# Where the matmuls' operands lie: the rows of x and h of an RWKV + gated-MLP kernel moved to multiples of 2048 bytes

## Chip, cores and metric

One Trainium2 chip, one of its cores. The metric is the device time of one execution in microseconds (us), inputs in HBM to output in HBM. Three runs of the kernel before took 540.85, 543.45 and 539.7 us; the median is 540.85.

## What is computed

An RWKV-style recurrence over 768 steps for 4 batches and 8 heads of 48 channels gives `y`; its heads side by side are the 384 channels of `x` for 3072 tokens, and a gated MLP of inner width 1536 follows. All in float32.

```python
for t in range(S):                                   # S = 768
    kt, vt, rt = k[:, :, t], v[:, :, t], r[:, :, t]
    cur = einsum('bhd,bhe->bhde', u[None] * kt, vt)
    y[:, :, t] = einsum('bhd,bhde->bhe', rt, state + cur)
    state = w[None, :, :, None] * state + einsum('bhd,bhe->bhde', kt, vt)
x = y.transpose(0, 2, 1, 3).reshape(3072, 384)
out = (sigmoid(x @ w_gate) * (x @ w_val)) @ w_out    # 384 -> 1536 -> 384
```

## The kernel before

**The recurrence** is done in 12 chunks of 64 tokens, each in two groups of heads (24 groups). A group's small matmuls (48 or 64 rows, 48 or 64 columns, float32) are those of `scores` (line 348), `outer` (L403) and `into_y` (L320); they read `chan`, `dec`, `toks`, `score` and `state`. Two chunks make a tile `xt` of 512 tokens; there are six tiles of tokens.

**Float32 by parts.** x, the weights and the inner h are each split into a high and a low part of type float32r (`x_high` L456 and `x_low` L460 on ScalarE and VectorE; `h_high` L520 on ScalarE, `h_low` L524 mostly on GpSimd; the weights once, L236 to L253). A product is then three matmuls (`PASS`): low weights with high x, high with high, high weights with low x.

**The MLP.** For each tile of tokens and each of 12 slices `f` of the inner width, `Moe.up` issues 18 matmuls (L502: gate and value, three k tiles, three passes) of a 128x128 weight and 512 columns of `xt` into a PSUM bank of the pool `ring`. Then come the sigmoid (L511, ScalarE), the product (L515, VectorE), `h_high` and `h_low`; and `Moe.down`, one slice later, issues 9 matmuls (L540) of 512 columns of `h` into the three banks `acc`. An item (one tile, one slice) is thus 27 large matmuls. The first tile's first two slices are done in halves of 256 columns; in the last tile the third output bank is done in two halves of 256 columns too (one of them in a bank named `sc`), 12 matmuls in `down` rather than 9. Every matmul has its own weight load (PEld in the profile), which runs beside the matmul ahead of it.

**Order.** The order of the first part is a table of steps written by hand (`START`); behind it a loop runs over the items and puts one group of the recurrence in at four slices of each tile (`SLOTS`). Nothing of it is touched by the change.

**Where the buffers lie.** SBUF has the same layout in all 128 partitions, and addresses here are bytes within one. Pools lie one behind the other in the order in which they are opened. In the program as built, the pools are `const` (small tables and masks, from 16512), `wp` (12 weight buffers of 9216 bytes, from 34336), `hp` (`sg`), `hq` (`h`, from 149024), `wtmp`, and then `ach` (`chan`), `atk` (`toks`), `adk` (`dec`) and `xp` (`xt`, from 196512). A row of `xt` is one k tile of one part, 512 values or 2048 bytes, and a row of `h` is one part of it, 2048 bytes too; one large matmul reads one such row in each partition. `const` ends at no multiple of 2048, so that no row does. The lines that say what a large matmul reads:

```python
xt[ti] = xp.tile([P, 4, 2, 512], F32R, name="xt")           # L442: k tile, part, column
h = self.h[f] = hq.tile([P, 2, 512], F32R, name="h")        # L519: part, column
o[:, self.cols], w[a][:, g * DM + kt * P : g * DM + (kt + 1) * P],   # L503, up
self.x[:, kt, b, self.cols], start=(k == 0), stop=(k == 8),          # L504
acc[:, to], w[a][:, 2 * DM + d * P : 2 * DM + (d + 1) * P],          # L541, down
h[:, b, cols], start=..., stop=...                                   # L542
```

A slow path behind the main one (an If on `flag`) is taken only where a decay lies outside 0.5 to 2; here it isn't.

Of the kernel before, what the change touches and what calls it, by code (L numbers as in the profile page):

```python
# [9 lines left out]
F32 = mybir.dt.float32  # L10
F32R = mybir.dt.float32r
I32 = mybir.dt.int32
# [7 lines left out]
P = 128  # L20
C = 64
# [3 lines left out]
CT = B * C  # L25
# [32 lines left out]
def rwkv_then_moe(ctx: ExitStack, tc: tile.TileContext, wd, ch, tk, rt, ut, wt, rk0, vn0, wd0, out):  # L58
    nc = tc.nc

    const = ctx.enter_context(tc.tile_pool(name="const", bufs=1))
    wp = ctx.enter_context(tc.tile_pool(name="wp", bufs=1))
    hp = ctx.enter_context(tc.tile_pool(name="hp", bufs=2))
    hq = ctx.enter_context(tc.tile_pool(name="hq", bufs=2))
    wtmp = ctx.enter_context(tc.tile_pool(name="wtmp", bufs=2))
    ps = ctx.enter_context(tc.tile_pool(name="ps", bufs=1, space=PSUM))
    ring = ctx.enter_context(tc.tile_pool(name="ring", bufs=3, space=PSUM))
# [1 line left out]
    main = ctx.enter_context(ExitStack())  # L69
    ach = main.enter_context(tc.tile_pool(name="ach", bufs=3))  # L70
    atk = main.enter_context(tc.tile_pool(name="atk", bufs=3))
    adk = main.enter_context(tc.tile_pool(name="adk", bufs=2))
    xp = main.enter_context(tc.tile_pool(name="xp", bufs=2))


    def two_banks():
# [2 lines left out]
    def one_bank():  # L79
        return ring.tile([P, 512], F32, name="ring")  # L80
# [7 lines left out]


    N2 = 2 * NP  # L90
    wu = const.tile([P, 2, N2], F32, name="wu")
    nc.sync.dma_start(out=wu, in_=wd)
    w = wu[:, 0]

# [10 lines left out]
        nc.sync.dma_start(out=toks[n], in_=tk[c, g])  # L105

    ub = const.tile([P, NG, 8 * D], F32, name="ub")
    gains = [const.tile([P, 8], F32, name=f"gain{i}") for i in range(2)]

    def load_receptance(n):  # L110
        c, g = GROUPS[n]
# [2 lines left out]
    def load_gains():  # L114
        nc.sync.dma_start(out=ub, in_=ut)

    later = const.tile([P, P], F32, name="later")
    same = const.tile([P, P], F32, name="same")

    masks = const.tile([P, 2, C], F32, name="masks")  # L120

    score = [const.tile([P, 512], F32, name=f"score{i}") for i in range(2)]

    state = const.tile([P, 4 * N2 * D // 2 + 16], F32, name="state")
    table = const.tile([P, 1], F32, name="table")

    def constants():
        nc.gpsimd.memset(same, 0.0)
# [21 lines left out]
    pw, tabk = every[:, :, 32:], every[:, :, 0:64]  # L150

    tabn = const.tile([P, N2, D], F32, name="tabn")
    flag = const.tile([1, 1], I32, name="flag")

    def power(lo, n, by):
        nc.vector.tensor_tensor(
# [47 lines left out]
            )  # L204

    def range_flag():
        good = const.tile([P, N2], F32, name="good")
        ones = const.tile([P, 1], F32, name="ones")
        total = const.tile([1, 1], F32, name="total")
        nc.vector.memset(ones, 1.0)  # L210
        nc.vector.tensor_tensor(good, w, pw[:, :, 1], ALU.is_equal)
        count = one_bank()
        nc.tensor.matmul(count[0:1, 0:N2], ones, good, start=True, stop=True)
        nc.vector.tensor_reduce(total, count[0:1, 0:N2], axis=mybir.AxisListType.X, op=ALU.add)
        nc.vector.tensor_scalar(flag, total, float(P * N2), None, ALU.is_lt)
# [38 lines left out]


    xt, dec, ga, yb, kv = {}, {}, {}, {}, {}
    seen = const.tile([112, 2], F32, name="seen")
    PP = [(p, p2) for p in range(2) for p2 in range(2)]
    QUARTERS = [(x, y) for x in range(2) for y in range(2)]

# [176 lines left out]
    def x_of(n, k):  # L437
        c, g = GROUPS[n]
        ti = TILE_OF[c]
        if ti not in xt:  # L440

            xt[ti] = xp.tile([P, 4, 2, 512], F32R, name="xt")  # L442
        co = CT * TILES[ti].index(c)
        return [
            (
                xt[ti][lo:hi, 2 * g : 2 * g + 2, k, co + 128 * be : co + 128 * be + 128],
                yb[n][be][lo:hi, 0:256].rearrange("q (p x) -> q p x", p=2),
            )

            for be in range(2)  # L450
            for lo, hi in (((0, 48), (64, 112)) if ti == 0 and g == 0 else ((0, 112),))
        ]

    def x_high(n):
        for x, y in x_of(n, 0):
            nc.scalar.copy(out=x, in_=y)  # L456

    def x_low(n):
        for (x, y), (hi, _) in zip(x_of(n, 1), x_of(n, 0)):
            nc.vector.tensor_tensor(x, y, hi, ALU.subtract)  # L460
# [164 lines left out]
    for step in START.split():  # L625
        name, _, arg = step.partition(".")
# [22 lines left out]
    for i in range(n0, len(items)):  # L649
        ti, h, f = items[i]  # L650
# [35 lines left out]
        if i == n0 + 11:  # L686
            range_flag()
# [7 lines left out]
    with tc.If(bad != 0):  # L695
        with ExitStack() as g:
            gp = g.enter_context(tc.tile_pool(name="gp", bufs=1))
# [21 lines left out]
            with tc.For_i(0, NC) as c:  # L719
# [38 lines left out]
                    out=xg[bass.ds(c, 1)].rearrange("o q p t -> (o q) p t"),  # L758
                    in_=yc.rearrange("q p b i -> q p (b i)"),
                )  # L760
            xr = gp.tile([P, 3, 2, CT], F32, name="xr")
            x = gp.tile([P, 3, 2, 512], F32R, name="xgr")
            with tc.For_i(0, NC, 2) as c:
                for j in range(3):
                    for to, lo, n, p in (
# [113 lines left out]
```

## Time and profile before

| | |
|---|---|
| median of three runs | 540.85 us (539.7 to 543.45) |
| profiled execution, first to last instruction (its span) | 538.6 us |
| PE busy (matmuls) | 519.2 us, 96% |
| PEld busy (weight loads) | 426.9 us, 79% |
| DVE, ACT, POOL busy | 218.3, 171.8, 175.0 us |
| mean granted TensorE clock | 0.996 of full |

The page gives the profiled execution's span alone; the difference of 2.2 us from the median is what lies around the first and the last instruction, and the scatter of the runs. A matmul's record lasts from its start to a modelled end, and successive records overlap; so the time from one start to the next, not a record's length, says what a matmul costs in a stream of them.

### The profile page before, as it was taken

Reading aid. Unit: us, or ns where it says so; the run is one execution under the profiler, and the core shown is the slowest. Engines: PE = TensorE matmul, PEld = TensorE weight load, DVE = VectorE, ACT = ScalarE, POOL = GpSimd, SP = SyncE. Lnnn points to the kernel's source line nnn. Section 1 sums busy time; section 2 is a strip of 40 time slices with the busy share of each in tenths; the row PEclk is TensorE's granted clock in tenths of the full one; section 3 lists DMA queues with packets and bytes.
Section 4 is the critical chain, followed back from the end, with each engine's and each line's share of the span. In section 5 each row is a group of like instructions: output and inputs, shape, how many; then the busy total and the mean of one; then the engine's idle time right before and its main releaser. Section 6 shows DMA issues by size and latency. Waiting matters only on the chain.

```text
span 538.6 us, 12067 instructions
## 1 busy us (share of the span) xinstructions
PE 519.2 (96%) x5268; PEld 426.9 (79%) x5268; DVE 218.3 (41%) x379; ACT 171.8 (32%) x358; POOL 175.0 (32%) x156
## 2 busy tenths in 40 slices
PE   4879999999999999999999999999999999999996
PEld 3769878788788887888888888888888887888885
DVE  7798999942343342432423414313414311111111
ACT  5576654522132232231332222222322212221121
POOL 3353330002814444234145144144242311111120
PEclk9999999999999999999999999999999999999999
DMA  8886903053022213220303402203300001100001
GB/s 324 314 301 239 382 2 99 16 204 128 2 86 86 70 48 141 85 84 3 95 3 104 145 7 79 67 28 106 144 1 16 12 1 19 60 0 1 0 1 63
DMA packets 15707, 48.03 MB, mean 89 GB/s; under 512 B 2369, under 2 KB 5057, under 8 KB 14241
## 3 DMA queue, kind: packets, MB, share of 16 engines
q1 hardware_dynamic: 15360, 46.81, 25.2%
q8 instruction: 43, 0.70, 0.5%
q10 hardware_dynamic: 288, 0.39, 0.2%
q14 instruction: 16, 0.12, 0.1%
HBM read 40.12 MB, written 4.72 MB: 83 GB/s over the span
## 4 chain that ended last, share of the span: by engine, by line
PE 91%; DVE 4%; DMA 3%; ACT 1%; issue 0%; SPq 0%; DVEq 0%; ACTq 0%
PE ring L502 55%; PE acc L540 27%; PE ring L320 5%; PE sc L348 2%; DMA toks<-in_tk 1%; DMA chan<-in_ch 1%; PE sc L403 1%; DMA wr<-in_wt 1%; DVE score L362 1%; PE sc L540 1%; DVE wf L243 1%; DVE wf L244 1%; DVE wx L253 0%; ACT wf L236 0%; DVE wf L242 0%
## 5 line engine op out<-in xcount | busy, mean ns | idle before, releaser
L502 PE MATMUL ring<-xt,wx 128*128 128x512 f32 (+1 forms) x1332 | 317.1, 392 | 2.1 <-ACT wx L250 1.7
L502 PEld LDWEIGHTS ring<-xt,wx 128*128 128x128 f32 x1332 | 247.4, 191 | 57.5 <-ACT wx L250 1.9
L524 POOL TENSOR_TENSOR h<-sg,h 128x512 fp32r<-128x512 f32 (+1 forms) x68 | 91.8, 1350 | 332.4 <-ACT h L520 326.5
L540 PE MATMUL acc<-h,wx 128*128 128x512 f32 (+1 forms) x666 | 160.9, 383 | 0.0
L515 DVE TENSOR_TENSOR sg<-ring,sg 128x512 f32<-128x512 f32 (+1 forms) x74 | 50.0, 676 | 272.7 <-PE ring L502 272.7
L540 PEld LDWEIGHTS acc<-h,wx 128*128 128x128 f32 x666 | 119.6, 188 | 24.3
L511 ACT ACTIVATE sg<-ring 128x512 f32<-128x512 f32 (+1 forms) x74 | 43.4, 586 | 181.2 <-PE ring L502 181.2
L520 ACT CAST h<-sg 128x512 fp32r<-128x512 f32 (+1 forms) x74 | 45.3, 612 | 109.0 <-DVE sg L515 109.0
L422 ACT ACTIVATE state<-state,every 112x96 f32<-112x96 f32 x80 | 23.5, 363 | 26.7 <-PE ring L320 26.7
L460 DVE TENSOR_TENSOR xt<-ring,xt 112x256 fp32r<-112x256 f32 (+1 forms) x52 | 19.9, 418 | 26.9 <-ACT xt L456 26.9
L301 POOL TENSOR_TENSOR dec<-chan,every 128x512 f32<-128x512 f32 x20 | 23.8, 1190 | 13.8 <-PE ring L320 5.9
L362 DVE COPY_PREDICATED score<-masks,sc 128x512 f32<-128x512 int32 x32 | 23.8, 743 | 0.9
L456 ACT CAST xt<-ring 112x256 fp32r<-112x256 f32 (+1 forms) x52 | 17.1, 372 | 17.2 <-PE ring L320 15.6
L320 PE MATMUL ring<-score,toks 64*64 64x64 f32 (+1 forms) x768 | 18.6, 230 | 4.0 <-DVE score L362 2.0
L311 POOL TENSOR_TENSOR toks<-toks,tabn 128x384 f32<-128x384 f32 x18 | 19.7, 1093 | 0.0
L320 PEld LDWEIGHTS ring<-score,toks 64*48 64x48 f32 (+1 forms) x768 | 15.3, 133 | 5.2 <-POOL dec L301 1.9
L250 ACT CAST wx<-wf 128x1152 fp32r<-128x1152 f32 (+1 forms) x13 | 14.1, 1084 | 15.1 <-DVE wf L244 15.1
L244 DVE SCALAR_TENSOR_TENSOR wf<-wr,wf 128x1152 int32<-128x1152 int32 (+1 forms) x13 | 18.4, 1415 | 0.5
L320 PEld LDWEIGHTS ring<-dec,state 48*48 48x48 f32 (+1 forms) x704 | 12.0, 127 | 7.4 <-issue 6.7
L348 PE MATMUL sc<-dec,chan 48*64 48x64 f32 x768 | 17.6, 231 | 0.1
L289 POOL TENSOR_TENSOR dec<-dec,toks 128x384 f32<-128x384 f32 x16 | 16.3, 1016 | 1.2
L243 DVE SCALAR_TENSOR_TENSOR wf<-wr,wf 128x1152 int32<-128x1152 int32 (+1 forms) x13 | 16.5, 1266 | 0.5
(62 smaller groups left out, 253.0 us busy)
## 6 DMA issues: line engine op xcount, KB each, us to landing
wr<-in_wt SPq DMA_DIRECT2D x11, 1152.0 KB, 8.7
chan<-in_ch SPq DMA_DIRECT2D x24, 512.0 KB, 4.5
toks<-in_tk SPq DMA_DIRECT2D x24, 400.0 KB, 4.9
out_y<-wf SPq DMA_DIRECT2D x16, 256.0 KB, 2.3
dec<-in_rt SPq DMA_DIRECT2D x16, 192.0 KB, 2.6
xt<-xt SPq DMA_DIRECT2D x30, 64.0 KB, 2.3
wr<-in_wt SPq DMA_DIRECT2D x2, 576.0 KB, 5.2
xt<-xt SPq DMA_DIRECT2D x12, 32.0 KB, 4.9
```

Of the source, the lines that this page charges most:

```text
L244: nc.vector.scalar_tensor_tensor(g, low, 29, g, ALU.logical_shift_right, ALU.bitwise_or)
L301: eng.tensor_tensor(v4(t[:, 0]), v4(chan[n][:, 0]), bc2(table_of(n)), ALU.mult)
L320: nc.tensor.matmul(yb[n][bank][64 * half : 64 * half + m, cs], lhsT, rhs, start=first, stop=stop, skip_group_check=True,)
L348: nc.tensor.matmul(sc[64 * gm : 64 * gm + 64, be ^ gm, o : o + C], kk[row, cs : cs + C], rr[row, cs : cs + C], start=True, stop=True,)
L362: nc.vector.copy_predicated(t.rearrange("q (b m i) -> q b m i", b=2, m=4), masks[:, m].bitcast(I32).unsqueeze(1).unsqueeze(1).broadcast_to ...
L422: nc.scalar.activation(st[:, p, s], st[:, p, s], AF.Copy, scale=pw[0:112, 4 * g + 2 * p + s, 64:65],)
L502: nc.tensor.matmul(o[:, self.cols], w[a][:, g * DM + kt * P : g * DM + (kt + 1) * P], self.x[:, kt, b, self.cols], start=(k == 0), stop=(k ...
L511: nc.scalar.activation(sg[:, c], self.pair[f][0][:, c], AF.Sigmoid)
L515: nc.vector.tensor_tensor(sg[:, c], self.pair.pop(f)[1][:, c], sg[:, c], ALU.mult)
L520: nc.scalar.copy(out=h[:, 0, c], in_=sg[:, c])
L524: eng.tensor_tensor(h[:, 1, c], self.sg.pop(f)[:, c], h[:, 0, c], ALU.subtract)
L540: nc.tensor.matmul(acc[:, to], w[a][:, 2 * DM + d * P : 2 * DM + (d + 1) * P], h[:, b, cols], start=(f == 0 and k == 0 and self.cols.start ...
```

## The change

The pools are opened in another order, and the small tiles of `const` move into a pool of their own. A tile `front` of 64 bytes that nothing uses makes that pool end at 18432, which is 9 x 2048. Behind it lie `xt` (2 x 16384 bytes), the weights (12 x 9216 bytes, which is 54 x 2048), `h`, `sg`, and then all others. The slow path takes its x from the same buffers.

```diff
+    small = ctx.enter_context(tc.tile_pool(name="small", bufs=1))
+    xp = ctx.enter_context(tc.tile_pool(name="xp", bufs=2))
+    wp = ctx.enter_context(tc.tile_pool(name="wp", bufs=1))
+    hq = ctx.enter_context(tc.tile_pool(name="hq", bufs=2))
+    hp = ctx.enter_context(tc.tile_pool(name="hp", bufs=2))
     const = ctx.enter_context(tc.tile_pool(name="const", bufs=1))
-    wp = ctx.enter_context(tc.tile_pool(name="wp", bufs=1))
-    hp = ctx.enter_context(tc.tile_pool(name="hp", bufs=2))
-    hq = ctx.enter_context(tc.tile_pool(name="hq", bufs=2))
+    small.tile([P, 16], F32, name="front")
     wtmp = ctx.enter_context(tc.tile_pool(name="wtmp", bufs=2))
...
-    xp = main.enter_context(tc.tile_pool(name="xp", bufs=2))
...
-    wu = const.tile([P, 2, N2], F32, name="wu")
+    wu = small.tile([P, 2, N2], F32, name="wu")
...
-            xt[ti] = xp.tile([P, 4, 2, 512], F32R, name="xt")
+            xt[ti] = xp.tile([P, 4, 2, 512], F32R, name="xt", tag="xt")
...
-            xr = gp.tile([P, 3, 2, CT], F32, name="xr")
-            x = gp.tile([P, 3, 2, 512], F32R, name="xgr")
+            xr = xp.tile([P, 3, 2, CT], F32, name="xr", tag="xt")
+            x = xp.tile([P, 3, 2, 512], F32R, name="xgr", tag="xt")
```

(`gain0`, `gain1`, `later`, `same`, `masks`, `table`, `flag`, `good`, `ones`, `total` and `seen` move from `const` to `small` as `wu` does.) Starts in the two programs as built, in bytes, and what is left of them by 2048 and by 512:

| buffer | before | by 2048 | by 512 | after | by 2048 | by 512 |
|---|---|---|---|---|---|---|
| `xt`, rows | 196512, 212896 | 1952 | 416 | 18432, 34816 | 0 | 0 |
| `h`, rows | 149024, 153120 | 1568 | 32 | 161792, 165888 | 0 | 0 |
| `wx`, weights | 34336 + 9216 f | 1568 or 544 | 32 | 51200 + 9216 f | 0 or 1024 | 0 |
| `sg` | 144928, 146976 | 1568 | 32 | 169984, 172032 | 0 | 0 |
| `score` | 21248, 23296 | 768 | 256 | 177152, 179200 | 1024 | 0 |
| `dec` | 188320, 192416 | 1952 | 416 | 221152, 225248 | 2016 | 480 |
| `chan` | 166432, ... | 544 | 32 | 199264, ... | 608 | 96 |

A weight of 128 columns is 512 bytes in each partition and starts at a multiple of 512 behind the start of `wx`. On each of the five engines the instructions stand in the same order before and after, and wait for the same engines and queues, up to the slow path; the addresses are all that differs.

## Rows read from the trace of the kernel before

**Rows 1.** The page's parts 1, 2 and 4: engines, granted clock, and chain that ended last.
```profile
PE 519.2 (96%) x5268; PEld 426.9 (79%) x5268; DVE 218.3 (41%) x379; ACT 171.8 (32%) x358; POOL 175.0 (32%) x156
...
PEclk9999999999999999999999999999999999999999
...
PE 91%; DVE 4%; DMA 3%; ACT 1%; issue 0%; SPq 0%; DVEq 0%; ACTq 0%
PE ring L502 55%; PE acc L540 27%; PE ring L320 5%; PE sc L348 2%; DMA toks<-in_tk 1%; DMA chan<-in_ch 1%; PE sc L403 1%; DMA wr<-in_wt 1%; DVE score L362 1%; PE sc L540 1%; DVE wf L243 1%; DVE wf L244 1%; DVE wx L253 0%; ACT wf L236 0%; DVE wf L242 0%
```

**Rows 2.** Busy time by engine in two stretches; counts in brackets, then granted clock and DMA.
```profile
60.00:110.00 50.00, 49.53 (x510) 40.11 (x509) 46.97 (x53) 24.80 (x41) 7.83 (x4) 1.00 0.27 92
110.00:518.00 408.00, 407.88 (x3621) 332.27 (x3620) 116.43 (x232) 103.81 (x220) 139.78 (x120) 1.00 0.18 59
```

**Rows 3.** Groups of instructions by line and shape: the large matmuls and their counts.
```profile
L502 PE MATMUL ring<-xt,wx 128*128 128x512 f32 x1260 | 304.6, 395 | 0.0
...
L540 PE MATMUL acc<-h,wx 128*128 128x512 f32 x594 | 152.6, 395 | 0.0
...
L540 PE MATMUL acc<-h,wx 128*128 128x256 f32 x72 | 14.8, 286 | 0.0
...
L502 PE MATMUL ring<-xt,wx 128*128 128x256 f32 x72 | 12.5, 343 | 2.1 <-ACT wx L250 1.7 <-DVE wx L253 0.5
...
L540 PE MATMUL sc<-h,wx 128*128 128x256 f32 x36 | 9.7, 279 | 0.0
```

**Rows 4.** PE in order of time, 100 to 121 us: start, length, line, count.
```profile
103.87 8.55 PE L502 MATMUL ring<-xt,wx 128*128 128x512 f32 x36
112.26 2.22 PE L540 MATMUL acc<-h,wx 128*128 128x512 f32 x9
114.32 4.35 PE L502 MATMUL ring<-xt,wx 128*128 128x512 f32 x18
118.51 2.22 PE L540 MATMUL acc<-h,wx 128*128 128x512 f32 x9
120.56 0.40 PE L502 MATMUL ring<-xt,wx 128*128 128x512 f32 x1
```

**Rows 5.** The same view from 100.42 us: two `down` blocks back to back.
```profile
100.25 3.79 PE L540 MATMUL acc<-h,wx 128*128 128x512 f32 x16
103.87 0.40 PE L502 MATMUL ring<-xt,wx 128*128 128x512 f32 x1
```

**Rows 6.** The same view at 48.7 us: halves of h, 256 columns each.
```profile
48.48 1.96 PE L540 MATMUL acc<-h,wx 128*128 128x256 f32 x15
50.28 0.39 PE L502 MATMUL ring<-xt,wx 128*128 128x512 f32 x1
```

**Rows 7.** Near 40 us: 12 halves of x from 40.03, the twelfth at 42.38; granted clock there.
```profile
40.03 2.76 PE L502 MATMUL ring<-xt,wx 128*128 128x256 f32 x12
...
42.38 0.59 PE L502 MATMUL ring<-xt,wx 128*128 128x256 f32 x2
...
39.90:42.60 2.70, 2.70 (x15) 0.50 0.91 342
```

**Rows 8.** PE in order of time in the last tile, 487 to 494 us.
```profile
487.44 4.34 PE L502 MATMUL ring<-xt,wx 128*128 128x512 f32 x18
491.62 0.75 PE L540 MATMUL acc<-h,wx 128*128 128x512 f32 x3
...
493.72 4.34 PE L502 MATMUL ring<-xt,wx 128*128 128x512 f32 x18
```

**Rows 9.** PE from 194.8 us: the small matmuls of one group.
```profile
195.28 0.65 PE L348 MATMUL sc<-dec,chan 48*64 48x64 f32 x32
195.75 0.58 PE L403 MATMUL sc<-toks 64*48 64x48 f32 x30
...
196.21 0.66 PE L320 MATMUL ring<-score,toks 64*48 64x64 f32 x30
196.80 2.32 PE L540 MATMUL acc<-h,wx 128*128 128x512 f32 x9
```

More of the change, by code (lines that the diff above doesn't have):

```diff
@@ L107, in rwkv_then_moe @@
     ub = const.tile([P, NG, 8 * D], F32, name="ub")
-    gains = [const.tile([P, 8], F32, name=f"gain{i}") for i in range(2)]
+    gains = [small.tile([P, 8], F32, name=f"gain{i}") for i in range(2)]
     def load_receptance(n):
@@ L115, in load_gains @@
         nc.sync.dma_start(out=ub, in_=ut)
-    later = const.tile([P, P], F32, name="later")
-    same = const.tile([P, P], F32, name="same")
-    masks = const.tile([P, 2, C], F32, name="masks")
+    later = small.tile([P, P], F32, name="later")
+    same = small.tile([P, P], F32, name="same")
+    masks = small.tile([P, 2, C], F32, name="masks")
     score = [const.tile([P, 512], F32, name=f"score{i}") for i in range(2)]
     state = const.tile([P, 4 * N2 * D // 2 + 16], F32, name="state")
-    table = const.tile([P, 1], F32, name="table")
+    table = small.tile([P, 1], F32, name="table")
     def constants():
@@ L152, in rwkv_then_moe @@
     tabn = const.tile([P, N2, D], F32, name="tabn")
-    flag = const.tile([1, 1], I32, name="flag")
+    flag = small.tile([1, 1], I32, name="flag")
     def power(lo, n, by):
@@ L206, in range_flag @@
     def range_flag():
-        good = const.tile([P, N2], F32, name="good")
-        ones = const.tile([P, 1], F32, name="ones")
-        total = const.tile([1, 1], F32, name="total")
+        good = small.tile([P, N2], F32, name="good")
+        ones = small.tile([P, 1], F32, name="ones")
+        total = small.tile([1, 1], F32, name="total")
         nc.vector.memset(ones, 1.0)
@@ L256, in rwkv_then_moe @@
     xt, dec, ga, yb, kv = {}, {}, {}, {}, {}
-    seen = const.tile([112, 2], F32, name="seen")
+    seen = small.tile([112, 2], F32, name="seen")
     PP = [(p, p2) for p in range(2) for p2 in range(2)]
```

## The prediction, made before the changed kernel ran

> **What bounds the kernel now.** I read the page's busy times and its chain first [rows 1]. TensorE is busy 96% of the span and makes up 91% of the chain that ended last, 55% with the large matmuls of `up` (L502) and 27% with those of `down` (L540). The clock is granted in full almost throughout. Then the two stretches [rows 2]: from 110 to 518 us PE is busy 407.88 of 408 us, while VectorE has 116, ScalarE 104 and GpSimd 140; only from 60 to 110 us is another engine near it, VectorE with 46.97 of 50. So nothing can be won behind 60 us by taking a wait away, and the change takes none: no instruction moves and no wait changes. What can move the time is the cost of one matmul in the stream, and for that I read starts in order of time, because records overlap.
>
> A row of 512 columns at the full clock of 2.4 GHz needs 512 / 2.4 = 213.3 ns if one column goes in per cycle. The trace has more:
>
> - x: 36 matmuls of `up` take 112.26 - 103.87 = 8.39 us, 233.1 ns each; the next 18 take 118.51 - 114.32 = 4.19 us, 232.8 [rows 4]. That is 20 ns over the columns.
> - h: 16 of `down` in a row take 103.87 - 100.25 = 3.62 us, 226.3 ns each [rows 5], 13 ns over. A `down` behind an `up` takes 2.06 or 2.05 us for nine [rows 4], 228.3 ns each: the first ones still go at x's pace.
> - h by halves: 15 take 50.28 - 48.48 = 1.80 us, 120.0 ns each [rows 6]. 256 columns need 106.7, so the excess is 13.3 ns again. It is a fixed part per matmul, not per column.
> - x by halves at half clock (0.50, that is 1.2 GHz): 11 steps in 42.38 - 40.03 = 2.35 us, 213.6 ns each [rows 7]; 256 columns need 213.3. At that clock the fixed part is gone.
>
> So x and h, which both are 2048-byte rows read against the same weights, cost 233 and 226.5 ns. The two differ in their bank, their order of passes and their address. Where they lie: a row of h begins 32 bytes behind a multiple of 512, exactly as each weight does; a row of x begins 416 behind one. Neither begins on a multiple of 64.
>
> **The change part by part.** Removed, added or moved instructions: none, so there is no cost of that kind, and the slow path isn't taken. What changes is four addresses.
>
> *x rows, from 416 behind a multiple of 512 to the multiple itself; the weights to it too.* After the change a row of x stands to the weight that is loaded beside it as a row of h stands to its weight before: at the same place within 512 bytes. If x then costs what h costs in a steady stream, 1260 matmuls [rows 3] gain 233.1 - 226.5 = 6.6 ns, 8.3 us. The trace doesn't show a row on a multiple of 64, so this is bounded from both sides: the most it can gain is the whole excess, 1260 x 19.8 = 24.9 us, since the half-clock rows show that it can be nothing; the most it can lose I take from the largest excess seen, below. I take 8.3 because it is the nearest row.
>
> *h rows, on the multiple of 2048.* Their place against the weights stays. What x no longer disturbs is the beginning of a `down`: 594 matmuls [rows 3], less the 72 of the last tile, gain 228.3 - 226.5 = 1.8 ns, 0.9 us. In the last tile 12 matmuls of `down` take 493.72 - 491.62 = 2.10 us [rows 8], where six at 226.5 and six at 120.0 would be 2.08: 12 x 0.02 = 0.2 us. The most that h can gain beyond is 594 x 13.2 = 7.8 us, and 180 halves [rows 3] x 13.3 = 2.4 us.
>
> *Everything else.* `dec`, `chan` and `score` move too, but no closer to or further from a multiple of 32. The small matmuls are about 2 us per group, and they don't show a price of the start: 32 that move `dec`, at 416 behind a multiple of 512, take 195.75 - 195.28 = 0.47 us, while 30 that move `score`, which begins on a multiple of 256, take 0.59 up to the next block [rows 9]. I cost them at nothing, within +-0.5 us. The operations of VectorE, ScalarE and GpSimd have their cover behind 110 us (the busiest has 140 of 408 [rows 2]); from 60 to 110 us VectorE has 3.0 us to spare. There some 200 large matmuls run; 5 ns each is 1.0 us and fits, 20 ns each would be 4 us and would not, so 1 us of a large gain would stay behind. The loads land in buffers that begin elsewhere; DMA is 3% of the chain [rows 1], 16 us, and 2% of that either way is 0.3 us.
>
> Sum: 8.3 + 0.9 + 0.2 = 9.4 us off. The profiled execution's span is 538.6, which becomes 529.2; with the 2.25 us by which the median of the runs lies over it, 540.85 - 9.4 = 531.5 us.
>
> **The rivals.**
>
> *A, the forecast:* x comes to h's pace, 531.5 us. For it: both are the same instruction, and h holds one pace to the nanosecond where its place against the weights is the same [rows 5, 6]. Against it: the order of passes and banks differ as well, and these stay.
>
> *B, no change:* 540.8 us. The excess belongs to float32r matmuls with a weight load each, and the 6.6 ns between x and h to the order in which banks or weights come. For it: it is the same 13.3 ns for 256 columns as for 512, as a fixed swap of weights would be; a half that spans a multiple of 2048 and one that doesn't are both in the 15 of [rows 6] at 120.0; and the small matmuls show no gain of aligned starts [rows 9]. The Trainium skill speaks for it: "SBUF — State Buffer", section "Door 1: The DMA port swizzle (why `[64,N]` ≈ `[32,N]`)", gives SBUF lines of 16 bytes, full speed where a line is used at least twice; all rows begin on multiples of 32 before, so by that rule nothing is left to win. The trace neither shows nor excludes that line.
>
> *C, the whole excess goes:* a row that begins askew costs a step more at its ends, and aligned rows don't. From A, the other 13.2 ns go of 1854 large matmuls and 13.3 of 180 halves: 24.5 + 2.4 = 26.9 us, less 1 us that VectorE keeps, 531.5 - 25.9 = 505.6 us at the end, some 518 if half goes. For it: 13.3 ns is 32 columns to the tenth, 128 bytes of a row, which is what one more piece of 128 bytes would cost a row that begins 32 bytes into one, for 256 and 512 columns alike. Against it: at half clock nothing is left of it, [rows 7], and [rows 9] show nothing like it. The Trainium skill has a price too, in "TensorE: Matmul & The Clock Gate", section "Back-to-back issue gap": N / 2.4 + 2.5 ns when warm, 215.8 for 512 columns, 17 under this trace's x. By it the 1854 would gain 1260 x 17.3 + 594 x 12.5 = 29.2 us, an estimate; no row here shows that gap.
>
> *D, slower:* after the change x, h and every weight begin on the same multiple of 512, and the reads of a row and of the next weight start together. If they then meet in the same part of SBUF, each matmul waits. Place: every large matmul behind 50 us. Price: x in the last tile costs (491.62 - 487.44) / 18 = 232.2 and the worst mean in the rows is x's 233.1; if h comes to that, 594 x 4.8 = 2.9 us; if x rises by as much as it lies over h now, 1260 x 6.6 = 8.3 us; together 552 us. It decides from 5.4 / 1854 = 2.9 ns more per matmul. Against it: h and its weights have that same relation now, and are the cheaper pair.
>
> **How the numbers follow.** A 0.37, B 0.34, C 0.14, D 0.15. A's own range is 528 to 536: x anywhere between 1 ns under and 3 ns over h's pace. A run of three tells about 1% from no change, 5.4 us. Faster by over 1% holds all of C and nearly all of A; slower by over 1% is D and a little that I have not thought of; within 1% is B and the low end of A: 0.48, 0.36 and 0.16. The range leaves out the lower half of C and the upper two thirds of D: 513 to 546 us.
>
> **What would show it.** In the changed kernel, first the starts in a stretch like [rows 4]: 18 matmuls of `up` in 4.08 us and nine of `down` in 2.04 are A, 4.19 and 2.05 are B, 3.9 and 1.95 are C, anything over 4.25 is D. The halves of h near 48 us show the fixed part by itself: 120 ns in A and B, under 115 in C. PE must stay busy all the time from 110 us on; if PE idles between 60 and 110 us with VectorE ahead of it, C came and met VectorE. I am wrong in the step on x if x keeps 233 while h keeps 226.5: then it is the order of passes or the banks, not the address, that sets them apart.

## The result, and the profile after

The changed kernel takes 533.4 us, the median of four runs (532.54 to 534.7), against 540.75 for the kernel before (also four runs, 539.7 to 543.45). The ratio is 0.9853, 95% interval 0.9822 to 0.9884: 1.5% faster. The forecast was 531.5 us, faster.

The page of the kernel after, the parts that answer to [rows 1] (its lines are two higher: `up` is L504, `down` L542):

```profile
span 530.5 us, 12067 instructions
...
PE 510.7 (96%) x5268; PEld 426.0 (80%) x5268; DVE 216.7 (41%) x379; ACT 171.7 (32%) x358; POOL 173.7 (33%) x156
...
PE ring L504 55%; PE acc L542 28%; PE ring L322 5%; PE sc L350 2%; PE sc L405 1%; DMA wr<-in_wt 1%; DVE wf L245 1%; DVE wf L246 1%; PE sc L542 1%; DVE wf L244 0%; DVE xt L462 0%; DVE sg L517 0%; DVE score L364 0%; ACT wx L252 0%; DVE toks L313 0%
```

The chain is the same in its large parts, and the counts are the same; PE's busy time falls by 8.5 us, and none of the others' by more than 1.6. Two stretches, columns as in [rows 2]:

```profile
60.00:110.00 50.00, 49.53 (x513) 40.74 (x512) 46.07 (x53) 25.29 (x41) 7.84 (x4) 1.00 0.24 81
110.00:510.00 400.00, 399.88 (x3618) 331.22 (x3617) 115.17 (x230) 102.27 (x218) 139.88 (x121) 1.00 0.18 58
```

PE is still busy without a gap behind 110 us, and VectorE still has 4 of 50 us to spare ahead of it. No wait came in. What changed is the pace. PE in order of time (start, length, line, count), as [rows 4, 5]:

```profile
101.97 8.32 PE L504 MATMUL ring<-xt,wx 128*128 128x512 f32 x36
110.13 2.20 PE L542 MATMUL acc<-h,wx 128*128 128x512 f32 x9
112.17 4.24 PE L504 MATMUL ring<-xt,wx 128*128 128x512 f32 x18
116.25 2.20 PE L542 MATMUL acc<-h,wx 128*128 128x512 f32 x9
```

36 of `up` take 110.13 - 101.97 = 8.16 us, 226.7 ns each, where they took 233.1; 18 take 4.08 (4.19), nine of `down` 2.04 (2.06 and 2.05). x goes at h's pace to the nanosecond. The same view at the halves of h, as [rows 6], and in the last tile, as [rows 8]:

```profile
47.77 1.48 PE L542 MATMUL acc<-h,wx 128*128 128x256 f32 x11
49.08 4.27 PE L504 MATMUL ring<-xt,wx 128*128 128x512 f32 x18
...
479.03 4.27 PE L504 MATMUL ring<-xt,wx 128*128 128x512 f32 x18
483.14 0.73 PE L542 MATMUL acc<-h,wx 128*128 128x512 f32 x3
...
485.22 1.55 PE L504 MATMUL ring<-xt,wx 128*128 128x512 f32 x6
```

Eleven halves of h take 49.08 - 47.77 = 1.31 us, 119 ns each; in the trace the first step is 117 ns and the other ten are 120, as before: the fixed part of 13 ns stays. In the last tile x costs (483.14 - 479.03) / 18 = 228.3 ns (232.2), and 12 of `down` 2.08 us (2.10).

### The profile page after: what moved, and what is told of

Read it like the earlier page. It is cut to its first block, busy times and chain, and to the rows that moved or that the text cites. A ratio compares the mean times of both kernels' runs of the same rounds, so it can differ in the third digit from the quotient of the medians.

```text
span 530.5 us, 12067 instructions
## 1 busy us (share of the span) xinstructions
PE 510.7 (96%) x5268; PEld 426.0 (80%) x5268; DVE 216.7 (41%) x379; ACT 171.7 (32%) x358; POOL 173.7 (33%) x156
## 4 chain that ended last, share of the span: by engine, by line
PE 92%; DVE 4%; issue 1%; DMA 1%; ACT 1%; POOL 0%; SPq 0%; DVEq 0%; ACTq 0%
PE ring L504 55%; PE acc L542 28%; PE ring L322 5%; PE sc L350 2%; PE sc L405 1%; DMA wr<-in_wt 1%; DVE wf L245 1%; DVE wf L246 1%; PE sc L542 1%; DVE wf L244 0%; DVE xt L462 0%; DVE sg L517 0%; DVE score L364 0%; ACT wx L252 0%; DVE toks L313 0%
## 5 line engine op out<-in xcount | busy, mean ns | idle before, releaser
L504 PE MATMUL ring<-xt,wx 128*128 128x512 f32 (+1 forms) x1332 | 308.6, 386 | 1.4 <-ACT wx L252 1.4
L504 PEld LDWEIGHTS ring<-xt,wx 128*128 128x128 f32 x1332 | 246.1, 190 | 50.4 <-ACT wx L252 1.6
L526 POOL TENSOR_TENSOR h<-sg,h 128x512 fp32r<-128x512 f32 (+1 forms) x68 | 89.5, 1316 | 323.7 <-ACT h L522 318.9
L542 PE MATMUL acc<-h,wx 128*128 128x512 f32 (+1 forms) x666 | 160.3, 382 | 0.0
L542 PEld LDWEIGHTS acc<-h,wx 128*128 128x128 f32 x666 | 119.5, 188 | 23.4
L303 POOL TENSOR_TENSOR dec<-chan,every 128x512 f32<-128x512 f32 x20 | 25.0, 1250 | 14.6 <-DMA chan<-in_ch 8.0
L246 DVE SCALAR_TENSOR_TENSOR wf<-wr,wf 128x1152 int32<-128x1152 int32 (+1 forms) x13 | 18.4, 1415 | 0.5
L350 PEld LDWEIGHTS sc<-dec,chan 48*64 48x64 f32 x768 | 15.4, 145 | 2.1 <-issue 1.3
L309 DVE TENSOR_TENSOR chan<-chan,every 128x512 f32<-128x512 f32 x24 | 16.7, 695 | 0.1
```

The source lines that it names most:

```text
L246: nc.vector.scalar_tensor_tensor(g, low, 29, g, ALU.logical_shift_right, ALU.bitwise_or)
L303: eng.tensor_tensor(v4(t[:, 0]), v4(chan[n][:, 0]), bc2(table_of(n)), ALU.mult)
L350: nc.tensor.matmul(sc[64 * gm : 64 * gm + 64, be ^ gm, o : o + C], kk[row, cs : cs + C], rr[row, cs : cs + C], start=True, stop=True,)
L504: nc.tensor.matmul(o[:, self.cols], w[a][:, g * DM + kt * P : g * DM + (kt + 1) * P], self.x[:, kt, b, self.cols], start=(k == 0), stop=(k ...
L526: eng.tensor_tensor(h[:, 1, c], self.sg.pop(f)[:, c], h[:, 0, c], ALU.subtract)
L542: nc.tensor.matmul(acc[:, to], w[a][:, 2 * DM + d * P : 2 * DM + (d + 1) * P], h[:, b, cols], start=(f == 0 and k == 0 and self.cols.start ...
```

## Experiments

Three theories of why x became as cheap as h. **R:** what counts is where a row begins against the weights. **M:** a row must itself begin on a multiple (64 or more, up to 2048). **S:** x and h must begin alike, whatever the weights do. In all rows below, the time of a block of 18 is the start of the block behind it less its own.

**x moved, not aligned.** The kernel before with one pool opened earlier (the slow path, which isn't taken, draws on it as in the change). The buffers behind x move by 32768 bytes, which is 16 x 2048, so that x's is the only place by 2048 that changes:

```diff
     hq = ctx.enter_context(tc.tile_pool(name="hq", bufs=2))
+    xp = ctx.enter_context(tc.tile_pool(name="xp", bufs=2))
...
-    xp = main.enter_context(tc.tile_pool(name="xp", bufs=2))
```

> The kernel before, with the x pool opened right behind h: x rows then begin 32 bytes behind a multiple of 512 as the weights and h do, and on no multiple of 64. Theory R (the place of a row against the weights, within 512 bytes, decides): up goes at 226.5 ns per matmul, 18 in 4.08 us, and the time is about 532 us. Theory M (a row must itself begin on a multiple of 64 or more): up stays at 233 ns, 18 in 4.19 us, 540.8 us. Theory S (x and h must begin alike; the weights don't matter): 226.5 ns, 532 us.

```profile
279.69 4.24 PE L502 MATMUL ring<-xt,wx 128*128 128x512 f32 x18
283.77 2.20 PE L540 MATMUL acc<-h,wx 128*128 128x512 f32 x9
285.81 4.24 PE L502 MATMUL ring<-xt,wx 128*128 128x512 f32 x18
```

533.55 us, ratio 0.9855 (0.9811 to 0.9899). `up` takes 4.08 us, `down` 2.04: the whole gain, with x at 1568 by 2048 and behind the weights. From the start of the first full `up` to that of the last `down` it is 475.23 us here and in the changed kernel, 483.10 in the kernel before. So x's place alone makes the gain; M falls, and so does "x must lie in front of the weights".

**The weights moved, x on multiples of 2048.** First with one toks buffer between x and the weights, then with two tiles:

```diff
+    mid = ctx.enter_context(tc.tile_pool(name="mid", bufs=1))
     wp = ctx.enter_context(tc.tile_pool(name="wp", bufs=1))
...
-    state = const.tile([P, 4 * N2 * D // 2 + 16], F32, name="state")
+    state = mid.tile([P, 4 * N2 * D // 2 + 16], F32, name="state")
...
-    every = const.tile([P, N2, 129], F32, name="every")
+    every = mid.tile([P, N2, 129], F32, name="every")
```

(with toks: a pool `atk0` of one buffer in that place, and two buffers left in `atk`.)

> The changed kernel, with one toks buffer (3200 bytes) put between x and the weights: x rows stay on multiples of 2048, weights and h begin 128 bytes behind a multiple of 512. Theory R: x goes back to 233 ns, 18 in 4.19 us, h behind it 228; about 541 us. Theory M: x stays at 226.5 ns, 533.4 us, at most h slows. Theory S: x and h begin differently, so x goes back to 233 ns, about 541 us.

> As the run with the weights moved, but with state and every between x and the weights in place of the toks buffer, so that no load waits otherwise than in the changed kernel: x on multiples of 2048, weights and h 96 bytes behind a multiple of 512. Theory R: x at 233 to 234 ns, h 228, 541 to 542 us. Theory S: the same. Theory M: x at 226.7 ns; h, no longer on a multiple of 64, at 233 at the worst: 533.4 to 537 us.

The first, then the second:

```profile
231.40 2.22 PE L543 MATMUL acc<-h,wx 128*128 128x512 f32 x9
233.46 4.35 PE L505 MATMUL ring<-xt,wx 128*128 128x512 f32 x18
237.65 2.22 PE L543 MATMUL acc<-h,wx 128*128 128x512 f32 x9
```

```profile
285.07 4.37 PE L505 MATMUL ring<-xt,wx 128*128 128x512 f32 x18
289.28 2.23 PE L543 MATMUL acc<-h,wx 128*128 128x512 f32 x9
```

x is back at 4.19 and 4.21 us on perfectly aligned rows. 545.4 us, ratio 1.007 (1.0046 to 1.0094), and 542.91 us, 1.0035 (1.0016 to 1.0053). The first is 4 us over what its pace explains: from the first full `up` to the last `down` it takes 483.08 us, as the kernel before does, but its first full `up` begins at 57.21 us, where the kernel before has 50.28. I put that down to the separate pool, in which one load of toks waits longer; the second run, without that pool, doesn't have it. Waits of the DMA queue in the first 60 us, in total, times, longest; the changed kernel, then the run with toks between:

```profile
SPq L107 <- PE ring L322: 9.4, 3, 6.3
```

```profile
SPq L108 <- PE ring L323: 21.7, 3, 11.0
```

**h alone moved.** `state` and `every` in a pool ahead of `hq` rather than of `wp`.

> The changed kernel, with the tiles state and every (7264 bytes) put between the weights and h: x and weights stay on multiples of 512, h begins 96 bytes behind one. Theory R (a row against the weights): x stays near 226.7 ns, 18 of up in 4.08 us, h goes to 233, nine of down in about 2.09 us instead of 2.04; 533.4 + 594 x 6 ns = about 537 us. Theory S (x and h must begin alike): both go to 233, about 544 us. Theory M (a row by itself must begin on a multiple of 64 or more): h goes to 233 and x stays, as R.

```profile
228.28 4.28 PE L505 MATMUL ring<-xt,wx 128*128 128x512 f32 x18
232.39 2.28 PE L543 MATMUL acc<-h,wx 128*128 128x512 f32 x9
234.51 4.28 PE L505 MATMUL ring<-xt,wx 128*128 128x512 f32 x18
```

538.7 us, ratio 0.9948 (0.9928 to 0.9968). `down` takes 2.12 us, 235.6 ns each, and x 4.11, 228.3: in the trace its first eight steps behind a `down` are uneven and the rest 226.7 ns, so it pays for its first matmuls behind h alone. S falls. The time is 2 us over R's 537 because I had priced h alone: with what x loses behind h, it is 481.14 us from the first full `up` to the last `down`, 5.9 more than in the changed kernel, and 533.4 + 5.9 = 539.3. The profiled execution is the slowest of the seven (541.17 us); in it, a wait for the fills of x near 38 us is followed by halves of `up` at half clock (mean granted clock from 39.98 to 47.60 us: 0.57), and its first full `up` begins 3.7 us later than the changed kernel's.

**The distance.** Two pools `xa` and `xb` of one buffer each, and small tiles of `small` moved behind the one or the other, so that one run has x at two distances:

```diff
-            xt[ti] = xp.tile([P, 4, 2, 512], F32R, name="xt", tag="xt")
+            xt[ti] = (xa, xb)[ti % 2].tile([P, 4, 2, 512], F32R, name="xt", tag="xt")
```

> The changed kernel with its two x buffers at 1408 and 1536 by 2048 (small tables moved behind them; weights and h stay on multiples of 512 and 2048): x of tiles 0, 2, 4 lies 384 bytes behind a multiple of 512, as it lay against the weights before, x of tiles 1, 3, 5 on one. Theory R: 233 ns in the even tiles, 226.5 in the odd ones, some 537.5 us. Theory M: 226.5 in both if multiples of 128 do (533.4 us), 233 in both if it takes 2048 (541 us). Theory S: as R.

> The changed kernel with its two x buffers 256 bytes (even tiles) and 384 bytes (odd tiles) behind a multiple of 512; weights and h on one. Theory R with a period of 512 bytes: both near 233 ns, 541 us. Theory R with a period of 256: even tiles 226.7, odd tiles 233, 537.5 us.

> The changed kernel with its two x buffers 448 bytes (even tiles) and 480 bytes (odd tiles) behind a multiple of 512; weights and h on one. Theory R as a matter of equal places: both near 233 ns, 541 us. If a distance of up to 64 bytes is as good as none: 226.7 ns in both, 533.4 us.

> The changed kernel with its two x buffers 192 bytes (even tiles) and 320 bytes (odd tiles) behind a multiple of 512; weights and h on one. Theory R with a period of 256 bytes and nothing good between: 233 ns in both, 541 us. If half a period is as good as none, neither of these shows it; what would is a place at 128, which cost 233 before.

> The changed kernel with its two x buffers at 1664 and 1952 by 2048: x of the even tiles 128 bytes behind a multiple of 512, x of the odd ones 416 behind one (1952, as in the kernel before). Weights and h stay. Theory R: both differ from the weights, both near 233 ns, 541 us. Theory M: 226.5 ns in the even tiles (a multiple of 128), 233 in the odd ones (no multiple of 64), 537.5 us. Theory S: as R.

For each of the five in this order, one `up` of an even tile and the block behind it, then one of an odd tile (two for the fourth run):

```profile
224.76 4.36 PE L507 MATMUL ring<-xt,wx 128*128 128x512 f32 x18
228.95 2.22 PE L545 MATMUL acc<-h,wx 128*128 128x512 f32 x9
...
322.70 4.24 PE L507 MATMUL ring<-xt,wx 128*128 128x512 f32 x18
326.78 2.20 PE L545 MATMUL acc<-h,wx 128*128 128x512 f32 x9
```

```profile
224.66 4.24 PE L507 MATMUL ring<-xt,wx 128*128 128x512 f32 x18
228.74 2.20 PE L545 MATMUL acc<-h,wx 128*128 128x512 f32 x9
...
322.12 4.35 PE L507 MATMUL ring<-xt,wx 128*128 128x512 f32 x18
326.31 2.22 PE L545 MATMUL acc<-h,wx 128*128 128x512 f32 x9
```

```profile
226.12 4.36 PE L507 MATMUL ring<-xt,wx 128*128 128x512 f32 x18
230.32 2.22 PE L545 MATMUL acc<-h,wx 128*128 128x512 f32 x9
...
331.21 4.36 PE L507 MATMUL ring<-xt,wx 128*128 128x512 f32 x18
335.41 2.23 PE L545 MATMUL acc<-h,wx 128*128 128x512 f32 x9
```

```profile
227.22 4.36 PE L507 MATMUL ring<-xt,wx 128*128 128x512 f32 x18
231.42 2.22 PE L545 MATMUL acc<-h,wx 128*128 128x512 f32 x9
...
325.85 4.36 PE L507 MATMUL ring<-xt,wx 128*128 128x512 f32 x18
330.05 2.24 PE L545 MATMUL acc<-h,wx 128*128 128x512 f32 x9
332.13 4.30 PE L507 MATMUL ring<-xt,wx 128*128 128x512 f32 x18
336.26 2.25 PE L545 MATMUL acc<-h,wx 128*128 128x512 f32 x9
```

```profile
227.48 4.36 PE L507 MATMUL ring<-xt,wx 128*128 128x512 f32 x18
231.67 2.22 PE L545 MATMUL acc<-h,wx 128*128 128x512 f32 x9
...
332.40 4.37 PE L507 MATMUL ring<-xt,wx 128*128 128x512 f32 x18
336.61 2.23 PE L545 MATMUL acc<-h,wx 128*128 128x512 f32 x9
```

| x's start less the weights', by 512 (by 256) | us for 18 | ns each |
|---|---|---|
| 0; 256 (0) | 4.08; 4.08 | 226.7 |
| 320 (64) | 4.13 or 4.20 | 229.4 or 233.3 |
| 384; 128 (128) | 4.19; 4.19 | 232.8 |
| 416 (160) | 4.21 | 233.9 |
| 192; 448 (192) | 4.20; 4.20 | 233.3 |
| 480 (224) | 4.20 | 233.3 |

The times, of one run each, are 537.07, 537.38, 540.96, 541.89 and 542.98 us. Distances that differ by 256 cost the same (0 and 256, 128 and 384, 192 and 448): the period is 256 bytes, not the 512 that I had read from the two buffers, and even 32 bytes short of it costs the full 6.6 ns. At 64 the pace depends on what went ahead: in the odd tile from 290 to 370 us four of the eight `up` ahead of a `down` take 4.14 us and four 4.20, the slow ones each behind the first `down` after a group of the recurrence. For h, the run with h moved has a distance of 96: 235.6 ns.

**Half the weight columns.** The last three ask what the remaining 13.3 ns are, and two of them move the weights' start without moving any buffer. The first of them has, in `up`:

```diff
-                            o[:, self.cols], w[a][:, g * DM + kt * P : g * DM + (kt + 1) * P],
+                            o[0:64, self.cols], w[a][:, g * DM + kt * P : g * DM + kt * P + 64],
```

and the others add 24 columns, or `24 * a` (`a` is 1 for the low weights), to both ends of the slice.

> The changed kernel with 64 of the 128 weight columns in up, so that a weight is 256 bytes in each partition; half of h is left out (sigmoid, product and the parts of h work on 64 partitions, down on 64 rows). It asks whose the remaining 13.3 ns per matmul are. If they go with the length of the weight load: up at 220 ns, 18 in 3.96 us. If they are fixed per matmul: 226.7, 18 in 4.08 us. Theory R expects no more than that, since x and weights begin alike.

> As the run with half the weight columns, but columns 24 to 88 of each weight in place of 0 to 64: no buffer moves, and every weight of up begins 96 bytes behind a multiple of 256, x on one. Theory R (the place against the weights within 256 bytes): up 6 to 7 ns per matmul slower than in that run, 18 in about 0.12 us more. Theory M (the row's own start): no difference.

> As the run with half the weight columns, but the low weights alone begin 96 bytes behind a multiple of 256. If a row is disturbed by the weight that is loaded beside it for the next matmul: the third of each three (high weights, low x, before a low weight) is slow. If by its own weights: the first of each three (low weights). On average a third of what all weights cost, some 2 ns per matmul, either way. Theory M: no difference.

The first and the seventeenth matmul of one block in each of the three, in this order (the seventeenth is the first of the second line):

```profile
121.86 4.13 PE L504 MATMUL ring<-xt,wx 128*64 128x512 f32 x17
...
125.59 0.40 PE L504 MATMUL ring<-xt,wx 128*64 128x512 f32 x1
```

```profile
122.09 4.29 PE L504 MATMUL ring<-xt,wx 128*64 128x512 f32 x18
...
125.77 0.61 PE L504 MATMUL ring<-xt,wx 128*64 128x512 f32 x2
```

```profile
121.87 4.13 PE L504 MATMUL ring<-xt,wx 128*64 128x512 f32 x17
...
125.60 0.40 PE L504 MATMUL ring<-xt,wx 128*64 128x512 f32 x1
```

Their whole times (556.93, 554.13 and 557.03 us, one run each) say nothing, since `down` works on 64 rows there and each change between the two shapes costs time of its own. Within the block, 16 steps take 3.73, 3.68 and 3.73 us, and the first step, 280 ns in each by the trace, still belongs to such a change. The other 15 are 230.0, 226.7 and 230.0 ns. Three things follow. The fixed part can be 13.3 ns with half the columns too, while a weight load's record shrinks from 188 to 134 ns (medians), so it doesn't go with the length of the weight load. The start of the weights by itself, with x and all buffers in place, moves the pace by 3.3 ns, which M excludes. But it moves it the other way than R said: with weights of 256 bytes the equal beginnings are the slower ones, and 96 bytes apart is as good as equal is for weights of 512. R holds as "the place against the weights counts", and falls as "equal is best". The third run is undecided: moving the low weights alone left the pace as it was, which fits neither of its two readings. In the blocks shown, the steps of the first and the third run are the same within 1 ns and repeat every six (between 224 and 236 ns), not every three as the passes do.

## Why the prediction was right, step by step

- *"What can move the time is the cost of one matmul in the stream".* Right: PE has no gap behind 110 us before or after, and no wait took the place of the gain. From the first full `up` block (50.28 in [rows 6], now 49.08) to the last matmul of `down` the stream is 483.10 - 475.23 = 7.9 us shorter; 1.2 us come from before it, and some 1 us goes behind it, with the last copies and stores. That makes 538.6 - 530.5 = 8.1 us of span. I take the 1.2 and the 1 for scatter between executions: the run with x behind h has the same stream, but its first full `up` at 50.55 us and 5.4 us behind its last `down` (before 5.2, after 6.2).
- *x, 6.6 ns on 1260 matmuls, 8.3 us.* Measured 6.4 ns in a block of 36 and 6.1 in one of 18, but 3.9 ns on the 216 of the last tile (232.2 to 228.3), where in the changed kernel the first five steps behind a `down` with halves are 229 to 236 ns: 1044 x 6.25 + 216 x 3.9 = 7.4 us (7.3 summed over the trace). I took all tiles for alike.
- *h, 0.9 us, and 0.2 in the last tile.* `down` behind an `up` went from 2.055 to 2.04 us; nine behind a group of the recurrence lost a little (2.16 us, now 2.18), and I had counted them as gaining. Some 0.6 us in all, by the sum over the trace. Small, and half of what I said.
- *Sum 9.4 us.* The stream gave 7.9, and the medians differ by 7.35. The two terms make up 1.5 of the 2.05 that are missing; the rest is within the scatter of the runs (532.54 to 534.7). The lower end of *A*'s own range, 528, was worked wrongly: 1 ns under h's pace on 1260 matmuls is 1.3 us, which makes it some 530.
- *The small matmuls, at nothing.* Right: from the first full `up` to the last `down` they take 40.02 us in both kernels. The 0.59 us of [rows 9], which I set against 0.47, holds the step of some 150 ns into the `down` behind it, so it showed no difference to begin with.
- *The place within 512 bytes.* The mechanism was right, its period wrong: 256. The two buffers of the kernel before, at distances 0 and 384, could not tell. That this didn't matter is luck: the change puts x at 0, which is best for either period. The rows ahead of the result hardly told A from B, which I gave 0.37 and 0.34, and the change by itself could not tell R from M and S; only the experiments do.
- *B* (no change, the lines of 16 bytes): all rows began on multiples of 32 before, and 32 bytes cost 6.6 ns. The Trainium skill's 16-byte lines ("SBUF — State Buffer", section "Door 1: The DMA port swizzle (why `[64,N]` ≈ `[32,N]`)") don't account for that; here the measurement decides. In the kernel before, the 18 steps of `up` from 114.32 us alternate between 224 to 230 and 234 to 238 ns, while the passes repeat every three, so the order of passes alone doesn't make the 6.6 ns either.
- *C* (the whole excess goes): the halves stayed at 119 to 120 ns, and no distance tried went below 226.7. By the Trainium skill ("TensorE: Matmul & The Clock Gate", section "Back-to-back issue gap") an isolated matmul of 512 columns takes 215.8 ns warm, an estimate from its formula, and the same section has some 131 for a stream with weight loads; the trace has 226.7 at best, for float32r with a weight load per matmul, and here the measurement decides.
- *D* (the same beginning makes the reads meet, and all slows): the reverse. With weights of 512 bytes the same beginning by 256 is the cheapest of the distances tried; whether reads meet at the others isn't shown.

## What to carry to other kernels

Where TensorE is busy without a gap, take starts from the trace in order of time, divide by the count, and compare two streams of the same shape: a few ns between them are a per cent of the kernel. If operands differ in cost, move one buffer by 32 to 128 bytes against the weights and read the starts again, in several blocks; it costs nothing in instructions. What helps is found by trying: here a distance of 0 by 256 bytes, with half the weight columns another one.

## What the runs showed of the hardware that I had not expected

- A float32r matmul of 512 columns with its own 128 x 128 weight load went at 226.7 ns where row and weights begin alike by 256 bytes, and at 229 to 236 ns at the other distances tried; at half clock the fixed part was gone [rows 7]. I read this as the row's and the next weight's reads getting in each other's way, which the runs make likely (the place of either one against the other moves the cost) but don't show directly.
- Where matmuls with weights of 128x64 and of 64x128 took turns, the step from one shape to the other took 315 to 328 ns from start to start and the step behind it 278 to 339, rather than 227 each.
